# A two-layer kernel whose second input projection takes seven block products instead of eight

## Chip, core and metric

One core of one Trainium2 chip runs one program. The metric is the device time of one launch in microseconds, the median of several runs; less is better. The engines are named as the profile names them: TensorE (PE, its weight loads PEld), VectorE (DVE), ScalarE (ACT), GpSimd (POOL) and SyncE (SP), which here only issues DMAs.

## What is computed

```python
def _attn_ref(x):                        # x: 2 x 3008 x 256
    X = np.fft.fft(x, axis=1)
    X = np.fft.fft(X, axis=2)
    return X.real.astype(np.float32)

def _moe_ref(x, w_in, w_out):            # x: 6016 x 256, w_in: 256 x 2048, w_out: 2048 x 256
    h = x @ w_in
    g = h * (1.0 / (1.0 + np.exp(-h)))
    return (g @ w_out).astype(np.float32)

def _moe2_ref(x, w_in, w_out):           # the same sizes
    h = x @ w_in
    relu6 = np.clip(h + 3.0, 0.0, 6.0)
    g = h * relu6 / 6.0
    return (g @ w_out).astype(np.float32)
```

The reference calls them one after the other: the real part of a two-dimensional Fourier transform, then two layers of two matrix products each. The weights come in as 64-bit floats.

## The kernel before

**Precision.** TensorE multiplies in `float32r`. Each operand is split into a high part (a copy to that type, on ScalarE) and a low part (the operand less the high part, on VectorE or GpSimd), and a product takes three matmuls: high x high, low x high, high x low (`mm3`, lines 243 to 245 in the profile of this kernel). Three such matmuls are called a triple below. All are of 128x128 weights and 502 moving columns (500 in the last chunk).

**Columns and chunks.** The Fourier transform uses the symmetry of a real input: it leaves, for each of 3010 pairs of frequencies, an even and an odd part (`eo`). The pairs are cut into six chunks of 502 (`CHUNKS`); a chunk stands for 2 x 502 tokens.

**Weights.** Each layer has eight pairs `g` of hidden blocks (`whi`, `wlo`: 2 x 512 columns for a pair, 256 of the input projection and 256 of the output projection for each block of 128 hidden units). They are decoded from the bits of the 64-bit floats in a chain of VectorE operations of 1024 columns (`bits_to_float32`). `decoder` and `stage` are generators that hand out one operation after another; `advance` takes from them as many as a credit in ns allows, once per unit, so VectorE's other work stands between them. In layer one `stage` also decodes the first four pairs of layer two, and keeps them in HBM (`w2_d`); the last 14 units of layer one load and split them; the other four are decoded in layer two.

**Layer one.** A unit is one chunk and one hidden block `f`: 96 units, in the order of `segs`, first a few blocks of each chunk (`PARTS`), since the weights are still being decoded, then the rest. `win1` makes the product of the even part into the PSUM tile `ab` (one triple), and VectorE puts `z` aside; `win1_end` adds the odd part's product on top (one triple), and VectorE makes the second half as 2z - ab. `parts` applies SiLU twice for each half on ScalarE, `low` makes the low parts `glo` on GpSimd, and `wout1` makes the output projection into four PSUM accumulators (four triples), three units later (`LAG`). `win1` is called one unit ahead of its `win1_end`. The results stay in SBUF (`y1`).

**Layer two.** A unit is one half of a chunk (502 tokens) and one pair of blocks: 96 units of 24 matmuls. `win2` makes four products (two blocks, two halves of the 256 input rows) into `hp`, of 1004 columns; ScalarE makes relu(h+3), VectorE takes the minimum with 6 and multiplies, ScalarE and VectorE split, and `wout2` follows three units later.

The order on each engine is the order in which this code issues instructions; nothing reorders them. Each engine takes its instructions in order, and one that waits holds up all behind it. All DMAs that matter go through SyncE's one queue.

## Time and profile before

| | |
|---|---|
| median of 3 runs | 996.31 us (993.98 to 997.43) |
| the profiled execution | 994.24 us |
| its span, first to last instruction | 992.5 us |
| mean granted clock of TensorE, of full | 0.993 |
| busy: PE, DVE, ACT, POOL | 975.0, 571.0, 525.1, 255.7 us |
| matmuls | 4416, of them 1152 into `hp` |

The span is one profiled execution; the 1.74 us around it are no part of the trace. The busy time of an engine says how full it is, and not whether anything waits for it; that is seen in the waits and in slices of the span.

### The profile page before, as it was taken

The numbers are of one execution on the slowest core, as the hardware profiler recorded it, in microseconds if no ns is written. First come the engines' busy times: TensorE is split into PE (matmuls) and PEld (weight loads), VectorE is DVE, ScalarE is ACT, GpSimd is POOL, SyncE is SP. The second block draws the span as 40 slices with busy tenths as digits, with TensorE's granted clock in tenths as the row PEclk, the third lists the DMA queues.
The fourth block names the chain that finished last, engine by engine and source line by source line (L and its number), as shares of the span: only waits on it lengthen the run. The fifth ranks groups of instructions, "written<-read, shape, count | busy, mean of one in ns | idle before, by whom it ended". The sixth has DMA issues, their size and how long they took to land.

```text
span 992.5 us, 11053 instructions
## 1 busy us (share of the span) xinstructions
PE 975.0 (98%) x4416; PEld 807.4 (81%) x4416; DVE 571.0 (58%) x630; ACT 525.1 (53%) x751; POOL 255.7 (26%) x197
## 2 busy tenths in 40 slices
PE   9969999999999999999999999999999999999998
PEld 8948778888888888888888888888888888888886
DVE  7787777766767543555976445554444444444433
ACT  3858666676565555665555444344443434444442
POOL 0046665666666666662000000000000000000000
PEclk9979999999999999999999999999999999999999
DMA  9411111001212000021100000000000000000000
GB/s 363 171 53 64 53 44 53 11 0 44 74 64 75 22 32 32 24 104 43 43 1 0 1 22 21 21 21 21 0 22 1 21 1 21 9 12 22 1 21 21
DMA packets 11007, 40.46 MB, mean 41 GB/s; under 512 B 1350, under 2 KB 6348, under 8 KB 8140
## 3 DMA queue, kind: packets, MB, share of 16 engines
q1 hardware_dynamic: 10812, 39.49, 11.0%
q8 instruction: 34, 0.56, 0.2%
q10 hardware_dynamic: 144, 0.27, 0.1%
q14 instruction: 17, 0.14, 0.0%
HBM read 31.48 MB, written 8.27 MB: 40 GB/s over the span
## 4 chain that ended last, share of the span: by engine, by line
PE 92%; DVE 2%; ACT 0%; issue 0%; DVEq 0%
PE y L245 18%; PE y L243 17%; PE y L244 17%; PE hp L245 9%; PE hp L243 9%; PE hp L244 9%; PE ab L245 4%; PE ab L243 4%; PE ab L244 4%; DVE lo L177 0%; DVE hi L175 0%; DVE z L473 0%; DVE h L484 0%; DVE lo L180 0%; DVE wlo L143 0%
## 5 line engine op out<-in xcount | busy, mean ns | idle before, releaser
L560 POOL TENSOR_TENSOR glo<-h,ghi 128x502 fp32r<-128x502 f32 (+1 forms) x192 | 255.3, 1351 | 199.5 <-PE y L244 116.9
L245 PE MATMUL y<-ghi,wlo 128*128 128x502 f32 (+1 forms) x768 | 301.0, 392 | 0.0
L243 PE MATMUL y<-ghi,whi 128*128 128x502 f32 (+1 forms) x768 | 300.9, 392 | 0.0
L244 PE MATMUL y<-glo,whi 128*128 128x502 f32 (+1 forms) x768 | 300.3, 391 | 0.0
L549 DVE SCALAR_TENSOR_TENSOR h<-h,hp 128x1004 f32<-128x1004 f32 (+1 forms) x96 | 115.2, 1200 | 259.3 <-ACT h L548 259.3
L548 ACT ACTIVATE h<-hp,three 128x1004 f32<-128x1004 f32 (+1 forms) x96 | 105.5, 1099 | 160.9 <-PE hp L245 150.2
L244 PEld LDWEIGHTS y<-glo,whi 128*128 128x128 f32 x768 | 145.8, 190 | 31.6
L243 PEld LDWEIGHTS y<-ghi,whi 128*128 128x128 f32 x768 | 145.3, 189 | 31.0
L245 PEld LDWEIGHTS y<-ghi,wlo 128*128 128x128 f32 x768 | 144.9, 189 | 30.6
L496 ACT ACTIVATE ghi<-h 128x1004 fp32r<-128x1004 f32 (+1 forms) x96 | 100.3, 1045 | 125.1 <-DVE h L549 125.1
L245 PE MATMUL hp<-uhi,wlo 128*128 128x502 f32 (+1 forms) x384 | 150.7, 392 | 0.0
L243 PE MATMUL hp<-uhi,whi 128*128 128x502 f32 (+1 forms) x384 | 150.1, 391 | 0.0
L244 PE MATMUL hp<-ulo,whi 128*128 128x502 f32 (+1 forms) x384 | 149.9, 390 | 0.0
L484 DVE SCALAR_TENSOR_TENSOR h<-z,ab 128x502 f32<-128x502 f32 (+1 forms) x96 | 65.0, 677 | 124.9 <-PE ab L245 113.5
L500 ACT ACTIVATE ghi<-ab 128x502 fp32r<-128x502 f32 (+1 forms) x96 | 56.5, 589 | 125.9 <-DVE h L484 125.8
L562 DVE TENSOR_TENSOR glo<-h,ghi 128x1004 fp32r<-128x1004 f32 (+1 forms) x96 | 114.9, 1197 | 0.0
L243 PE MATMUL ab<-xhi,whi 128*128 128x502 f32 (+1 forms) x192 | 76.2, 397 | 10.7 <-DVE z L473 9.9
L244 PEld LDWEIGHTS hp<-ulo,whi 128*128 128x128 f32 x384 | 72.7, 189 | 15.8
L243 PEld LDWEIGHTS hp<-uhi,whi 128*128 128x128 f32 x384 | 72.3, 188 | 15.3
L245 PEld LDWEIGHTS hp<-uhi,wlo 128*128 128x128 f32 x384 | 72.2, 188 | 15.2
L473 DVE SCALAR_TENSOR_TENSOR z<-eb,w_sb,ab 128x502 f32<-128x502 f32 (+1 forms) x96 | 70.8, 738 | 11.8 <-PE ab L245 1.5
L245 PE MATMUL ab<-xhi,wlo 128*128 128x502 f32 (+1 forms) x192 | 75.9, 395 | 0.9 <-DVE wlo L143 0.9
(92 smaller groups left out, 820.9 us busy)
## 6 DMA issues: line engine op xcount, KB each, us to landing
raw<-in_w SPq DMA_DIRECT2D x16, 1024.0 KB, 4.8
x<-in_xh SPq DMA_DIRECT2D x6, 1024.0 KB, 7.1
out<-y SPq DMA_DIRECT2D x20, 251.0 KB, 2.1
eb<-e_d SPq DMA_DIRECT2D x10, 251.0 KB, 3.3
w_d<-ta SPq DMA_DIRECT2D x4, 512.0 KB, 3.0
w<-w_d SPq DMA_DIRECT2D x4, 512.0 KB, 3.8
x<-in_xh SPq DMA_DIRECT2D x3, 512.0 KB
out<-y SPq DMA_DIRECT2D x4, 250.0 KB, 2.0
```

The lines of the kernel that those rows point to most:

```text
L243: T.matmul(o, wh, xhi, start=first, stop=False, **group)
L244: T.matmul(o, wh, xlo, start=False, stop=False, **group)
L245: T.matmul(o, wl, xhi, start=False, stop=last, **group)
L473: V.scalar_tensor_tensor(out=z[:, :n], in0=eb[:, :n], scalar=w128_sb[:, f : f + 1], in1=ab[:, :n], op0=ALU.mult, op1=ALU.add)
L484: V.scalar_tensor_tensor(out=h[:, 0, :n], in0=z[:, :n], scalar=2.0, in1=ab[:, :n], op0=ALU.mult, op1=ALU.subtract)
L496: A.activation(ghi[:, :, :n], h[:, :, :n], AF.Copy)
L500: A.activation(ghi[:, s, :n], src, AF.Silu)
L548: A.activation(h[:, :, :n], hp[:, :, :n], AF.Relu, bias=three)
L549: V.scalar_tensor_tensor(out=h[:, :, :n], in0=h[:, :, :n], scalar=6.0, in1=hp[:, :, :n], op0=ALU.min, op1=ALU.mult)
L560: G.tensor_tensor(out=glo[:, s, :n], in0=h[:, s, :n], in1=ghi[:, s, :n], op=ALU.subtract)
L562: V.tensor_tensor(out=glo[:, :, :n], in0=h[:, :, :n], in1=ghi[:, :, :n], op=ALU.subtract)
```

## The change

**Layer two's input projection.** A unit is now a whole chunk (both halves of 502 tokens) and a pair of blocks: 48 units (`units2`). The 2x2 block product (two hidden blocks by two halves of the input rows, times two halves of the rows by two halves of the tokens) is made from seven products instead of eight, with sums of blocks on both sides. The weight sums (`s1` to `s4`) are made in `block_sums`; those of the moving side (`t1` to `t4`) in `moving`, once per chunk, by VectorE, and split by ScalarE and GpSimd. The products go into four single PSUM tiles, `pa`, `pb`, `pc`, `pd`. `pa` gets three products one after the other, and ScalarE copies it to SBUF after each (`p1`, `u2`, `u3`); `pb` gets two. VectorE adds the pieces together in PSUM. Between the products stand triples of `y` (the output projection of the unit before), handed out by `fill`; a unit has 7 + 8 triples in the order `pa`, `pc`, 2 `y`, `pb`, `pa`, `y`, `pd`, `y`, `pa`, 4 `y`, `pb`. All four low parts of a unit are made on GpSimd.

**Weights.** Six pairs are decoded, summed and split in layer one and wait in HBM in three pieces; the last two are done in units 2 to 8 of layer two.

**Layer one.** `win1` runs two units ahead (`AHEAD`), and `z` has room for four. At the start `wout1` follows two units later instead of three (`CLOSE`). The low part of one half goes to VectorE for odd blocks. The credit per unit is 1500 throughout, instead of 1150 from the fourth on. Partial and full results of a chunk go to HBM and back (`part_d`, `y1_d`).

```diff
+RING = 10
+NEAR = 4
+FIRST = 4
 EARLY = 2
-STAGED = 4
+AHEAD = 2
+CLOSE = 5
+STAGED = 6
...
+    def block_sums(t, x):
+        V.tensor_tensor(out=x[:, 0:128], in0=t[:, 1, 0:128], in1=t[:, 1, 128:256], op=ALU.add)
+        V.tensor_tensor(out=t[:, 1, 0:128], in0=t[:, 0, 0:128], in1=t[:, 1, 0:128], op=ALU.subtract)
+        V.tensor_tensor(out=x[:, 128:256], in0=x[:, 0:128], in1=t[:, 0, 0:128], op=ALU.subtract)
+        V.tensor_tensor(out=x[:, 256:384], in0=t[:, 0, 128:256], in1=x[:, 128:256], op=ALU.subtract)
...
     def add_w2(t, a):
         V.tensor_tensor(out=t, in0=a, in1=t, op=ALU.add)
         yield 1200
+        block_sums(t, a[:, 0])
+        yield 1000
...
+            lows = t.bitcast(F32R), a[:, 0, 0:384].bitcast(F32R)
+            V.tensor_tensor(out=lows[0], in0=t, in1=h, op=ALU.subtract)
+            V.tensor_tensor(out=lows[1], in0=a[:, 0, 0:384], in1=a[:, 1, 0:384], op=ALU.subtract)
+            for dst, src in zip(w2_d[g], (h.bitcast(F32), t, a[:, :, 0:384])):
+                nc.sync.dma_start(dst, src)
...
+            A.activation(h, t, AF.Copy)
+            A.activation(a[:, 1, 0:384].bitcast(F32R), a[:, 0, 0:384], AF.Copy)
...
     def load_w2(g):
-        raws[g] = dp.tile([P, 2, 512], F32, name=f"w2_{g}", tag="raw")
-        nc.sync.dma_start(raws[g], w2_d[g])
-
-    def split_w2(g):
+        if not wx:
+            wx.append(eop.tile([P, NF // 2, 2, 384], F32R, name="wx", tag="eo"))
         weight_tiles(2, g)
-        split(whi[2, g], wlo[2, g], raws.pop(g))
+        for dst, src in zip((whi[2, g], wlo[2, g], wx[0][:, g]), w2_d[g]):
+            nc.sync.dma_start(dst.bitcast(F32), src)
...
+        i = units.index((k, f))
+        if i < 4:
+            if i % 2 == 0:
+                spare[0] = pools[0].tile([P, 2, CHUNK], F32R, name=f"zg{i}", tag="glo").bitcast(F32)
+            return spare[0][:, i % 2]
+        if i == 4:
+            spare[0] = stp.tile([P, 4, CHUNK], F32, name="zs", tag="su", bufs=1)
+        elif i == turn:
+            spare[0] = dp.tile([P, 4, 512], F32, name="zr", tag="raw")
+        return spare[0][:, i % 4]
...
-        z = pools[0].tile([P, CHUNK], F32, name="z", tag="z", bufs=1)
-        product(ab[:, :n], w(1, f, 0), (hi[:, 0, :n], lo[:, 0, :n]), True)
+        z = even_part(k, f)
+        product(ab[:, :n], w(1, f, 0), (hi[:, 0, :n], lo[:, 0, :n]))
...
         glo = pools[0].tile([P, 2, CHUNK], F32R, name="glo", tag="glo")
-        if segs[k][0] == 1:
-            for s in (1, 0):
-                G.tensor_tensor(out=glo[:, s, :n], in0=h[:, s, :n], in1=ghi[:, s, :n], op=ALU.subtract)
-        else:
-            V.tensor_tensor(out=glo[:, :, :n], in0=h[:, :, :n], in1=ghi[:, :, :n], op=ALU.subtract)
+        for s, eng in ((1, G), (0, V if f % 2 else G)):
+            eng.tensor_tensor(out=glo[:, s, :n], in0=h[:, s, :n], in1=ghi[:, s, :n], op=ALU.subtract)
...
                     if fs[0] == 0:
                         A.activation(dst, src, AF.Copy)
                     else:
                         V.tensor_tensor(out=dst, in0=dst, in1=src, op=ALU.add)
...
+                        credit[0] -= 400
+                yield
...
-                pools[1] = tc.alloc_tile_pool(name="psS", bufs=2, space=PSUM, side="right", reuse_waits="tile")
...
+    def moving(k):
...
+        st = stp.tile([P, 2, 2 * CHUNK], F32, name=f"u{k}", tag="su", bufs=1)
+        nc.sync.dma_start(st[:, :, : 2 * n], y1_d[j])
...
+        def rest(name, src):
...
+            G.tensor_tensor(out=lo, in0=src, in1=hi, op=ALU.subtract)
...
+        V.tensor_tensor(out=b12, in0=b22, in1=b12, op=ALU.subtract)
+        high("t1", b11)
+        yield
+        rest("t1", b11)
...
+        V.tensor_tensor(out=b21, in0=b11, in1=b21, op=ALU.subtract)
+        high("t2", b11)
+        yield
...
+
+    def fill(times=1):
+        for _ in range(times):
+            while waiting and next(waiting[0], waiting) is waiting:
+                waiting.pop(0)
...
-        if i >= LAG:
-            k_, f_ = units[i - LAG]
-            (wout1 if segs[k_][0] == 1 else wout2)(k_, f_)
+        lag = LAG - (i < CLOSE)
+        if i >= lag and i != CLOSE:
+            for _ in wout1(*units[i - lag]):
+                pass
+        if EARLY <= i < n1 - AHEAD:
+            win1(*units[i + AHEAD])
...
-        if f == fs[len(fs) // 2 - 1] and k + 1 < len(segs) and k + 1 not in xs:
-            l_, j_, _ = segs[k + 1]
-            xs[k + 1] = split_eo(j_) if l_ == 1 else split_y(j_)
-        if 2 <= i < turn:
-            spare()
...
+        if f == fs[len(fs) // 2] and fs[0]:
+            load_part(k)
+        if k + 1 < len(segs) and k + 1 not in xs and f == fs[1 if k + 2 == len(segs) else len(fs) // 2 - AHEAD]:
+            xs[k + 1] = split_eo(k + 1, segs[k + 1][0])
+        if 2 <= i < turn - AHEAD - 1:
+            advance(steps, 1500)
+        else:
...
+            q, odd = divmod(i - turn, 2)
+            if not odd and 0 <= q < STAGED - 1:
+                load_w2(q)
...
+    def high_part(g, h, i, n):
+        A.activation(g[0][:, i, :n], h[:, i, :n], AF.Copy)
+
+    def low_part(g, h, i, n):
+        G.tensor_tensor(out=g[1][:, i, :n], in0=h[:, i, :n], in1=g[0][:, i, :n], op=ALU.subtract)
...
+    for e, (k, f) in enumerate(units2):
+        j, fs = segs2[k]
+        n = CHUNKS[j][1]
+        u = us[k]
+        while f >= STAGED and len(finished) <= NF + 2 * (f - STAGED):
+            drive(steps2)
+        if e == 0:
+            go(ready, 8)
+        left = len(fs) - 1 - (f - fs[0])
+        more = k + 1 < len(segs2)
+        wh, wl = (t[2, f] for t in (whi, wlo))
+        xl, xh = (wx[0][:, f, i] for i in range(2))
+        a11, a12, s3, a22 = ((wh[:, i, 128 * c : 128 * c + 128], wl[:, i, 128 * c : 128 * c + 128]) for i in range(2) for c in range(2))
+        s1, s2, s4 = ((xh[:, 128 * i : 128 * i + 128], xl[:, 128 * i : 128 * i + 128]) for i in range(3))
+        pa, pc = (pools[1].tile([P, 512], F32, name=f"p{q}", tag=f"p{q}") for q in "ac")
+        product(pa[:, :n], a11, u["b11"])
+        product(pc[:, :n], a12, u["b21"])
+        hy, gy = split_tiles()
+        p1 = snapshot("p1", n)
+        if before:
+            before = (*before, hy, gy)
+            relu(hy, 0, before[3], before[2])
+        fill(2 if e else 4)
+        pb = pools[1].tile([P, 512], F32, name="pb", tag="pb")
+        product(pb[:, :n], s1, u["t1"])
+        V.tensor_tensor(out=pc[:, :n], in0=p1[:, :n], in1=pc[:, :n], op=ALU.add)
+        if before:
+            finish_last(before)
+            before[4][0, 1] = gy, 0
+            waiting.append(wout2(before[0], before[1], before[4]))
+        relu(hy, 1, pc, n)
+        times(hy, 1, pc, n)
+        product(pa[:, :n], s2, u["t2"], False)
+        u2 = snapshot("u2", n)
+        high_part(gy, hy, 1, n)
+        low_part(gy, hy, 1, n)
+        if e > 1:
+            advance(steps2, 1600 if e < FIRST else 2600)
+        if f == fs[0] and e:
+            go(ready, 1)
+        if left == 3 and more:
+            ready = moving(k + 1)
+            next(ready)
+        if more and left < 3:
+            go(ready, (2, 2, 3)[left])
+        fill(1)
+        pd = pools[1].tile([P, 512], F32, name="pd", tag="pd")
+        product(pd[:, :n], a22, u["t4"])
+        fill(1)
+        product(pa[:, :n], s3, u["t3"], False)
+        hx, gx = split_tiles()
+        u3 = snapshot("u3", n)
+        V.tensor_tensor(out=pc[:, :n], in0=u3[:, :n], in1=pb[:, :n], op=ALU.add)
+        V.tensor_tensor(out=pd[:, :n], in0=u3[:, :n], in1=pd[:, :n], op=ALU.subtract)
+        for op in (relu, times):
+            op(hx, 0, pc, n)
+            op(hx, 1, pd, n)
+        for op in (high_part, low_part):
+            op(gx, hx, 0, n)
+            op(gx, hx, 1, n)
+        if more and left == 0:
+            go(ready, 2)
+        fill(4)
+        product(pb[:, :n], s4, u["b22"], False)
+        V.tensor_tensor(out=pd[:, :n], in0=u2[:, :n], in1=pb[:, :n], op=ALU.add)
+        if e == 0:
+            load_w2(STAGED - 1)
+        elif e == 1:
+            begin(2, STAGED)
+        blocks = {(0, 0): (gy, 1), (1, 1): (gx, 0), (1, 0): (gx, 1)}
+        before = (k, f, n, pd, blocks)
```

What moves on the engines is shown at three places. Tile names carry the numbers that the program gives them.

VectorE in an ordinary stretch of layer two, before: `h` is the product with 6.0 taken as minimum, `glo` a low part, `ulo` a low part of a moving operand.

```order
L168 TENSOR_TENSOR ulo5_5146<-y1_619,uhi5_5145 128x1004
L549 SCALAR_TENSOR_TENSOR h_5182<-h_5182,hp_5181 128x1004
L562 TENSOR_TENSOR glo_5198<-h_5149,ghi_5150 128x1004
L549 SCALAR_TENSOR_TENSOR h_5214<-h_5214,hp_5213 128x1004
L562 TENSOR_TENSOR glo_5230<-h_5182,ghi_5183 128x1004
```

And in one unit after:

```order
L863 TENSOR_TENSOR pd_4986<-u2_4972,pb_4959 128x502
L824 TENSOR_TENSOR pc_5034<-p1_5044,pc_5034 128x502
L737 SCALAR_TENSOR_TENSOR h_5041<-h_5041,pd_4986 128x502
L737 SCALAR_TENSOR_TENSOR h_5041<-h_5041,pc_5034 128x502
L851 TENSOR_TENSOR pc_5034<-u3_5089,pb_5053 128x502
L852 TENSOR_TENSOR pd_5076<-u3_5089,pd_5076 128x502
L737 SCALAR_TENSOR_TENSOR h_5086<-h_5086,pc_5034 128x502
L737 SCALAR_TENSOR_TENSOR h_5086<-h_5086,pd_5076 128x502
```

Where a half-unit had two operations of 1004 columns, a unit has eight of 502, four of them sums into the PSUM tiles `pc` and `pd`, and no low parts.

TensorE at the beginning of layer one, before: the end of a unit's products into `ab_629`, then `ab_654`, the first that needs the second weight pair (`whi1_1`, `wlo1_1`), and behind it the first output projection (`y00`; three more triples follow).

```order
L243 MATMUL ab_629<-xhi1_533,whi1_0_499 128x502
L244 MATMUL ab_629<-xlo1_534,whi1_0_499 128x502
L245 MATMUL ab_629<-xhi1_533,wlo1_0_500 128x502
L243 MATMUL ab_654<-xhi1_533,whi1_1_642 128x502
L244 MATMUL ab_654<-xlo1_534,whi1_1_642 128x502
L245 MATMUL ab_654<-xhi1_533,wlo1_1_643 128x502
L243 MATMUL y00_663<-ghi_562,whi1_0_499 128x502
L244 MATMUL y00_663<-glo_620,whi1_0_499 128x502
L245 MATMUL y00_663<-ghi_562,wlo1_0_500 128x502
```

And after, the last two triples of that output projection, the product that needs the second pair (`ab_686`), and the end of the products into `ab_633`:

```order
L293 MATMUL y10_666<-ghi_588,whi1_0_525 128x502
L294 MATMUL y10_666<-glo_652,whi1_0_525 128x502
L295 MATMUL y10_666<-ghi_588,wlo1_0_526 128x502
L293 MATMUL y11_667<-ghi_588,whi1_0_525 128x502
L294 MATMUL y11_667<-glo_652,whi1_0_525 128x502
L295 MATMUL y11_667<-ghi_588,wlo1_0_526 128x502
L293 MATMUL ab_686<-xhi1_559,whi1_1_680 128x502
L294 MATMUL ab_686<-xlo1_560,whi1_1_680 128x502
L295 MATMUL ab_686<-xhi1_559,wlo1_1_681 128x502
L293 MATMUL ab_633<-xhi1_559,whi1_0_525 128x502
L294 MATMUL ab_633<-xlo1_560,whi1_0_525 128x502
L295 MATMUL ab_633<-xhi1_559,wlo1_0_526 128x502
```

The twelve matmuls into `y` stand ahead of the product that needs the new pair, and the triple that stood ahead of it stands behind.

GpSimd's end before: the low parts of the last units of layer one.

```order
L560 TENSOR_TENSOR glo_3811<-h_3763,ghi_3764 128x500 x2
L560 TENSOR_TENSOR glo_3836<-h_3799,ghi_3800 128x500 x2
L560 TENSOR_TENSOR glo_3879<-h_3830,ghi_3831 128x500 x2
L798 UNCONDITIONAL_BRANCH
L798 ISA
```

And after, at a change of chunk in layer two: `glo` is a low part of the hidden values, the others are low parts of the next chunk's moving sums (`t2`, `t4`, `t3`, `b22`).

```order
L745 TENSOR_TENSOR glo_6682<-h_6680,ghi_6681 128x502 x2
L645 TENSOR_TENSOR t2_5_6711<-u5_6453,t2_5_6711 128x502
L745 TENSOR_TENSOR glo_6731<-h_6729,ghi_6730 128x502 x2
L645 TENSOR_TENSOR t4_5_6714<-u5_6453,t4_5_6714 128x502
L645 TENSOR_TENSOR t3_5_6745<-u5_6453,t3_5_6745 128x502
L745 TENSOR_TENSOR glo_6776<-h_6774,ghi_6775 128x502 x2
L645 TENSOR_TENSOR b22_5_6748<-u5_6453,b22_5_6748 128x502
L745 TENSOR_TENSOR glo_6819<-h_6817,ghi_6818 128x502 x2
```

GpSimd works through layer two, and at a change of chunk four more operations stand among its low parts.

## Rows read from the trace of the kernel before

**Rows 1.** The page's first part: busy time, share of the span, instructions.

```profile
PE 975.0 (98%) x4416; PEld 807.4 (81%) x4416; DVE 571.0 (58%) x630; ACT 525.1 (53%) x751; POOL 255.7 (26%) x197
```

**Rows 2.** Windows by stage: stretch, length, busy us (instructions) per engine, granted clock, DMA share, GB/s.

```profile
148.62:463.90 315.28, 314.49 (x1377) 259.35 (x1378) 191.43 (x242) 193.76 (x333) 195.50 (x150) 1.00 0.12 42
...
200.00:300.00 100.00, 100.00 (x439) 82.41 (x438) 67.94 (x86) 62.73 (x109) 64.93 (x50) 1.00 0.13 45
...
464.00:988.50 524.50, 524.50 (x2294) 431.90 (x2292) 266.69 (x242) 234.27 (x234) 0.00 (x0) 1.00 0.04 15
```

**Rows 3.** TensorE's waits: who for whom, us in total, times, longest.

```profile
PE ab L243 <- DVE z L473: 9.9, 5, 3.4
...
PE ab L245 <- DVE wlo L143: 0.9, 1, 0.9
```

**Rows 4.** Timeline of TensorE, 52 to 67 us: start, duration, line, tiles [idle before].

```profile
52.44 0.49 PE L243 MATMUL ab<-xhi,whi 128*128 128x502 f32 x1 [0.80 <-DVE z L473]
...
56.68 0.50 PE L243 MATMUL ab<-xhi,whi 128*128 128x502 f32 x1 [2.60 <-DVE z L473]
...
62.18 0.79 PE L243 MATMUL ab<-xhi,whi 128*128 128x502 f32 x1 [3.38 <-DVE z L473]
...
66.66 0.79 PE L245 MATMUL ab<-xhi,wlo 128*128 128x502 f32 x1 [0.90 <-DVE wlo L143]
```

**Rows 5.** Windows of 5 and 10 us in layer one's beginning.

```profile
60.00:65.00 5.00, 2.08 (x4) 1.29 (x5) 4.86 (x8) 3.15 (x5) 2.56 (x3) 0.50 0.20 51
...
110.00:120.00 10.00, 8.09 (x36) 6.42 (x35) 8.37 (x9) 7.51 (x14) 6.47 (x5) 1.00 0.23 92
...
140.00:150.00 10.00, 8.76 (x39) 6.91 (x38) 8.65 (x9) 6.32 (x11) 7.18 (x6) 1.00 0.31 106
```

**Rows 6.** Groups of instructions by form: shapes, count | busy us, mean ns | idle before.

```profile
L560 POOL TENSOR_TENSOR glo<-h,ghi 128x502 fp32r<-128x502 f32 x160 | 213.8, 1358 | 175.9 <-PE y L244 97.7 <-ACT h L501 78.2
...
L562 DVE TENSOR_TENSOR glo<-h,ghi 128x1004 fp32r<-128x1004 f32 x80 | 95.8, 1198 | 0.0
...
L496 ACT ACTIVATE ghi<-h 128x1004 fp32r<-128x1004 f32 x80 | 83.6, 1045 | 104.9 <-DVE h L549 104.9
...
L484 DVE SCALAR_TENSOR_TENSOR h<-z,ab 128x502 f32<-128x502 f32 x80 | 54.1, 677 | 105.1 <-PE ab L245 94.5 <-issue 6.7 <-POOL glo L560 3.6
...
L501 ACT ACTIVATE h<-ab 128x502 f32<-128x502 f32 x80 | 46.8, 585 | 0.0
...
L117 DVE SCALAR_TENSOR_TENSOR lo<-raw,lo 128x1024 f32<-128x1024 uint32 x10 | 14.4, 1443 | 0.2
...
L586 DVE TENSOR_TENSOR y<-y,y 128x502 f32<-128x502 f32 x20 | 13.0, 675 | 0.0
```

**Rows 7.** Timeline of layer two, 703 to 705 us, three engines.

```profile
703.14 0.40 PE L245 MATMUL hp<-uhi,wlo 128*128 128x502 f32 x1
...
703.62 1.10 ACT L548 ACTIVATE h<-hp,three 128x1004 f32<-128x1004 f32 x1 [2.09 <-PE hp L245]
...
704.76 1.20 DVE L549 SCALAR_TENSOR_TENSOR h<-h,hp 128x1004 f32<-128x1004 f32 x1 [2.07 <-ACT h L548]
```

**Rows 8.** Timelines of VectorE and GpSimd: alone and beside each other.

```profile
56.54 0.68 DVE L175 TENSOR_TENSOR hi<-hi,lo 128x512 f32<-128x512 f32 x1
...
113.73 3.34 POOL L560 TENSOR_TENSOR glo<-h,ghi 128x502 fp32r<-128x502 f32 x2 [0.53 <-ACT h L501]
...
114.18 1.76 DVE L175 TENSOR_TENSOR hi<-hi,lo 128x512 f32<-128x512 f32 x1
...
207.09 2.52 POOL L560 TENSOR_TENSOR glo<-h,ghi 128x502 fp32r<-128x502 f32 x2 [1.61 <-PE y L244]
```

**Rows 9.** The end's timeline, and DMA issues: count, KB each, median us to landing.

```profile
988.84 0.59 ACT L610 ACTIVATE y<-y 128x500 f32<-128x500 f32 x1 [0.78 <-PE y L245]
...
w_d<-ta SPq DMA_DIRECT2D x4, 512.0 KB, 3.0
...
out<-y SPq DMA_DIRECT2D x4, 250.0 KB, 2.0
```

More of the change, by code (lines that the diff above doesn't have):

```diff
@@ new lines, in go @@
+    def go(steps, times):
+        for _ in range(times):
+            next(steps, None)
+    waiting = []
+    def fill(times=1):
+        for _ in range(times):
+            while waiting and next(waiting[0], waiting) is waiting:
+                waiting.pop(0)
+    ready = None
+    for i in range(n1):
+        k, f = units[i]
+        j, fs = segs[k]
+        if i >= EARLY:
+            win1_end(k, f)
+        if i >= 1:
+            low(*units[i - 1])
+        lag = LAG - (i < CLOSE)
[4 more added lines that the diff above has]
+            win1(*units[i + AHEAD])
@@ L669, in body @@
-    for p in (pools[1], psB, pools[0], xsp, eop, yp, dr, dp, wp, per):
+            q, odd = divmod(i - turn, 2)
+            if not odd and 0 <= q < STAGED - 1:
+                load_w2(q)
+        if i == n1 - 1:
+            load_raw(2, w2, STAGED)
+            load_raw(2, w2, STAGED + 1)
+        if i == n1 - 15:
+            ready = moving(0)
+            next(ready)
+        if i >= n1 - 12:
+            next(ready, None)
+    do_later()
+    low(*units[-1])
+    pools[1].release()
+    pools[1] = tc.alloc_tile_pool(name="psS", bufs=1, space=PSUM, side="right", reuse_waits="tile")
@@ new lines, in body, with relu, times @@
+    waiting += [wout1(*units[i]) for i in range(n1 - LAG, n1)]
+    def relu(h, i, c, n):
+        A.activation(h[:, i, :n], c[:, :n], AF.Relu, bias=three)
+    def times(h, i, c, n):
+        V.scalar_tensor_tensor(
+            out=h[:, i, :n], in0=h[:, i, :n], scalar=6.0, in1=c[:, :n], op0=ALU.min, op1=ALU.mult
+        )
+    def high_part(g, h, i, n):
+        A.activation(g[0][:, i, :n], h[:, i, :n], AF.Copy)
+    def low_part(g, h, i, n):
+        G.tensor_tensor(out=g[1][:, i, :n], in0=h[:, i, :n], in1=g[0][:, i, :n], op=ALU.subtract)
@@ L670, in body @@
+    hy, gy = split_tiles()
+    before = (*before, hy, gy)
+    relu(hy, 0, before[3], before[2])
+    finish_last(before)
+    before[4][0, 1] = gy, 0
+    waiting.append(wout2(before[0], before[1], before[4]))
+    while waiting:
+        fill()
+    for p in (pools[1], psB, pools[0], xsp, eop, xq, stp, dr, dp, wp, per):
         p.release()
```

318 lines of the change are left out of this document (172 added, 146 removed).

## The prediction

> **What bounds the kernel now.** I read the page's head first: TensorE is busy 975.0 us, 98% of the span [rows 1]. A busy share alone proves little, so I cut the span into stages [rows 2]: from 200 to 300 us TensorE never pauses and issues 439 matmuls in 100 us, 0.2278 us each; from 464 us to the last matmul at 988.4 it is busy all the time too. So **the price of a matmul here is 0.2278 us, of three that make one product ("a triple") 0.683 us**, and whatever removes matmuls without opening gaps shortens the span by that much each. In those stages VectorE has work for 267 of 524 us, ScalarE for 234 and GpSimd for none: there is room beside TensorE. Then I asked what TensorE waits for at all [rows 3]: 9.9 us in five waits for `z` on VectorE, 0.9 for a weight's low part. The timeline [rows 4] puts 6.8 us of these before 63 us, where the first weights are still being decoded; with TensorE busy for 2.1 of 5 us the granted clock stands there at 0.50 of full, the lower of its two levels, 1.2 GHz. The rest is in the slices 110 to 120 (1.9 us not busy) and 140 to 150 (1.2 us) [rows 5].
>
> **What the change removes.** Of the 4126 rows that TensorE has in the order, 3982 are left: 144 matmuls fewer. That is one product of eight in each of 48 units (8 x 3 x 48 = 1152 matmuls, seven eighths of them left). 144 x 0.2278 = **32.8 us**. Nothing else shrinks; TensorE's operands stay 128x128 weights against 502 columns, so the price per matmul stays.
>
> **What it adds in layer two.** A unit (one pair of hidden blocks, both halves of a chunk) is now 15 triples, 10.25 us, where two units of 5.47 stood. By width and source I price each operation [rows 6]: reading 502 columns from PSUM on ScalarE 0.585 us (the snapshots `p1`, `u2`, `u3` and four `relu`), a copy of 502 out of SBUF at most 0.56 (half of 1.045, and some fixed part), the VectorE products with 6.0 clipped 0.677, GpSimd's low parts 1.28 to 1.36. Per unit: ScalarE 3 x 0.585 + 4 x 0.585 + 4 x 0.56 = 6.3 us; VectorE 4 adds and 4 products = 5.4; GpSimd 4 x 1.3 = 5.2; all below 10.25. The one operation that no row shows is VectorE's add *into* PSUM (`pc`, `pd`). Its nearest row is the add of PSUM and SBUF into SBUF, 0.675 us; I take that, and keep twice it as the other end.
>
> Shares don't settle it, since every engine works in order and the pieces hang on each other. So I walked one unit. An engine starts 0.25 us after a triple's nominal end (the last matmul of `hp` starts at 703.14, ends its 0.228 at 703.37, ScalarE starts at 703.62) and 0.05 after another engine's end [rows 7]. Three chains matter. From the end of the third product into `pa` to the last product into `pb`: 0.25 + 0.585 + 0.675 and two changes of engine, 1.6 us, with four triples of `y` (2.73) to cover it. From the same end to the next unit's product into `pc`: snapshot, add, `relu`, product, 2.9 us, of six triples (4.10). And the longest, once round the unit to the next third product: 0.25, snapshot 0.585, adds 0.675 + 0.675, `relu` 0.585, product 0.677, add 0.675, snapshot 0.585, add 0.675, product 0.677, copy 0.56, `relu` 0.585, snapshot 0.585, with seven changes of engine: **8.1 us, of 14 triples, 9.57**. Each has over a microsecond left: 0 for an ordinary unit. The `y` triples that fill these places belong to the unit before, and their operands are ready about a unit early.
>
> The Trainium skill, Perfetto Trace Analysis (Optimizing Scalar/DVE Operations), gives VectorE a fixed part of some 125 ns on PSUM and 60 on SBUF; by that the add into PSUM would cost at most 0.065 us over its row, an estimate, and the longest chain 8.4 us: the sum would be the same. No run shows it yet.
>
> At a **change of chunk** GpSimd has a queue of its own: after the high parts of the last unit it makes two `glo` halves, `t4`, `t3`, two `glo` halves and `b22` in one row, seven operations. They begin some 3.6 us after the third product (0.25, snapshot, add, `relu`, product, copy and changes of engine) and `b22` is wanted 19 triples and one matmul after it, 13.2 us. Seven at 1.26 (a pair takes 2.52, [rows 8]) end at 12.4, at the mean of 1.358 at 13.1: 0 to little. Six changes: I put 0.5 us for all, up to 5.
>
> **The last two weight pairs** are decoded on VectorE in units 2 to 8: six operations of 1024 columns, at most 1.44 each, the four sums of 128 columns (0.3 each, an estimate: under half of the 0.675 for 502) and two low parts (1.2 and, for 384 columns, 0.5), 11.5 us per pair at most, 3.3 a unit. VectorE is free for about 3.0 us between its second product and the add after `u3`, and the first chain has 1.1 more. On average it fits; where the credit lets one more operation of 1.2 in, 0.4 us is lost, in some three or four units: **+1.5 us** (0 to 8).
>
> **Layer one.** The even parts are begun two units ahead, so VectorE has 6 triples (4.1 us) for `z` instead of 4 (2.7): 1.4 us more. Of the later waits, 1.9 and 1.2 us, 1.4 + 1.2 go: **-2.6** (0 to -3.1). At the start, the first 12 `y` matmuls now stand ahead of the product that waits for a weight's low part until 66.66 us [rows 4], and three matmuls that stood ahead of it now stand behind. TensorE thus does nine matmuls more in time that was idle: 9 x 0.228 = **-2.0** (0 to -3.8 at half the clock). The decoding itself, which ends the wait, is as long as before.
> Against that VectorE gets 48 of GpSimd's 192 low parts (48 x 0.68 = 33 us) and the staging of six pairs instead of four (2 x 8.7, six times 2.9 for sums and low parts, less four splits of 1.2: 29 us). 191.4 of 315.3 us [rows 2] becomes 253, 80%. With 4.1 us of slack for each `z`, and 12 us between a unit's first products and its `y`, I put 0. SyncE's queue carries some 38 MB more (layer one's results through HBM, the pairs in three pieces) at a DMA share that was 0.12 and 0.04, each load issued at least two units ahead of its use: 0.
>
> **The end.** The last copy of 0.59 us stays; the last store is 500 KB in one instead of 250. The nearest rows are 2.0 us for 250 KB and 3.0 for 512 [rows 9]: **+0.9**. The ten triples behind the last unit cover its tail.
>
> **Sum:** -32.8 - 2.0 - 2.6 + 0.5 + 1.5 + 0.9 = -34.5. The profiled execution took 994.24 us (span 992.5 and 1.74 around it): 959.7. The median of the runs, 996.31, lies 2.1 higher; a median of the changed kernel should lie somewhat above its own profile too. I forecast **961 us**.
>
> **Rivals.**
> *Longer links in layer two.* If the add into PSUM costs 1.0 us and each change of engine 0.15, the longest chain grows by 4 x 0.325 + 7 x 0.1 = 2.0 and passes its 9.57 by 0.57: 27 us in 48 units, 988; milder mixes 968 to 988. For it: no row shows the add. Against: every row with PSUM in it lies at 0.58 to 0.74 for 502 columns.
> *VectorE binds layer one.* Alone, the sum of 512 columns takes 0.68 us; beside GpSimd's two low parts it took 1.76 and those 3.34 instead of 2.52 [rows 8]: they exclude each other. The change lets the two halves of a low part start on both engines together, 48 times. At 1.1 us more each, VectorE's 253 us become 305 of 315, and where a unit needs 4.3 us instead of 4.1 for some 70 units, TensorE waits 14 us: 974. Against: GpSimd is busy less, and the credits even it out. The Trainium skill, SBUF — State Buffer (Who interferes with whom), says just that: a VectorE operation with two SBUF inputs and a GpSimd operation that reads SBUF block each other for the whole instruction. The trace agrees, with 1.76 against 0.68 us.
> *Slower than before.* One mechanism: the add into PSUM. Its four places in the longest chain leave 1.4 us; 34.5 us are used up when each unit passes by 0.72 more, at (1.4 + 0.72) / 4 = 0.53 over the row, an add of 1.2 us. At twice the row, 1.35, the chain passes by 1.3: 61 us, 1021.
>
> **Chances.** Forecast (952 to 968) 0.72; longer links 0.10; VectorE in layer one 0.10; slower 0.05; else 0.03. The range, 952 to 976, holds the first, most of the third and a part of the second, 0.8. Within 0.3%, about what a measurement of this kernel can tell from no change, lies almost nothing: faster 0.93, same 0.02, slower 0.05.
>
> **What would show it.** Right: TensorE at 438 or 439 matmuls per 100 us through layer two, about 492 us for its 48 units; no waits for `z` after 100 us; snapshots and products at their rows; the add into PSUM below 0.9 us. Wrong: TensorE waiting in each unit at the product into `pb` or the third into `pa` (longer links), at odd units of layer one for `z` (VectorE), at `b22` on GpSimd at each change of chunk, or VectorE's adds above 1.2 us.

## The result and the profile after

The changed kernel takes **966.14 us** (median of 4 runs, 965.61 to 966.29), the kernel before 996.15 beside it: a ratio of 0.970, interval 0.9682 to 0.9718. The forecast was 961, within 952 to 976. The profiled execution took 966.29 us (span 964.5), 27.95 less than that of before; the sum had 34.5. One of the four executions of the experiment with the even credit alone ran at a granted clock of 0.75 throughout (1151.03 us); its rows are left out, and without it that run's median is 962.79 us instead of 962.88.

The page's first part, of the kernel after (against [rows 1]):

```profile
PE 943.3 (98%) x4272; PEld 779.4 (81%) x4272; DVE 678.8 (70%) x924; ACT 643.3 (67%) x1122; POOL 532.5 (55%) x390
```

TensorE is as full as before, with 144 matmuls fewer; VectorE went from 58% to 70%, GpSimd from 26% to 55%. Windows by stage of the kernel after, as [rows 2] (stretch, length, busy us and instructions of PE, PEld, DVE, ACT, POOL, granted clock, DMA share, GB/s):

```profile
148.62:449.00 300.38, 298.47 (x1305) 245.55 (x1304) 252.37 (x308) 193.87 (x340) 174.11 (x117) 1.00 0.36 132
200.00:300.00 100.00, 99.65 (x436) 81.94 (x435) 93.27 (x109) 66.64 (x114) 58.33 (x38) 1.00 0.39 143
500.00:580.00 80.00, 75.08 (x317) 59.96 (x316) 61.53 (x84) 52.38 (x90) 44.10 (x33) 0.98 0.04 14
...
555.00:560.00 5.00, 2.57 (x9) 1.77 (x8) 4.71 (x8) 1.81 (x3) 1.65 (x2) 0.85 0.00 0
560.00:565.00 5.00, 5.00 (x20) 4.02 (x19) 2.62 (x4) 3.22 (x7) 3.70 (x3) 0.81 0.00 0
...
580.00:959.40 379.40, 379.34 (x1662) 312.77 (x1660) 205.26 (x319) 262.81 (x447) 227.95 (x180) 1.00 0.07 25
```

From 580 us to the last matmul, 379.4 us, TensorE never stops: 0.2283 us a matmul (0.2286 in the last row of [rows 2]). **What is missing stands in the third row**: in 80 us from 500 on it issues 317 matmuls, where 351 go through when nothing waits (first experiment). The waits of TensorE after (who for whom, us in total, times, longest; [rows 3] before):

```profile
PE pb L293 <- DVE pc L851: 4.9, 4, 2.4
PE ab L293 <- DVE zg L525: 2.4, 2, 1.8
PE y L293 <- ACT st L613: 1.8, 2, 1.6
PE y L293 <- ACT eo L401: 1.7, 1, 1.7
PE y L293 <- DVE st L615: 1.7, 2, 1.4
...
PE ab L293 <- DVE zs L525: 0.7, 2, 0.5
```

The waits for `z` (`zg`, `zs`) fell from 9.9 to 3.1 us. Three kinds are new. At the start of layer one `y` waits once for `eo`, for a place in PSUM that ScalarE empties (1.7 us). Later it waits for `st`: the accumulators of the chunk that just ended aren't empty yet (3.5 us). In layer two the second product into `pb` waits for `pc`, VectorE's sum, which reads `pb` first (4.9 us, all between 513 and 572 us).

The sum, stage by stage. The first product of layer two starts at 449.0 instead of 453.1, with 2076 matmuls ahead of it in both traces.

| term | predicted | measured |
|---|---|---|
| 144 matmuls fewer | -32.8 | -32.8 |
| layer one: start -2.0, `z` -2.6, VectorE 0 | -4.6 | -4.1 (453.1 to 449.0) |
| ordinary units | 0 | 0 (after 580 us) |
| changes of chunk | +0.5 | 0 alone (no wait after 580 us) |
| decoding the last two pairs | +1.5 | +7.7 ((351 - 317) x 0.2278) |
| last matmul to the span's end | +0.9 | +1.1 (964.5 - 959.30 against 992.5 - 988.41) |
| sum | -34.5 | -28.1, the profiled executions differ by 27.95 |

The row of layer one is good to about 1 us. Two experiments below (the second and the sixth) leave layer one as the change has it, and from the first product into `ab` to layer two's first product their traces have 403.1 and 403.0 us, the changed kernel's 402.1, that of before 406.4: 3.3 to 4.3 less.

**The operation that no row showed.** One line's operations (ns min/median/max, first and last start), after:

```profile
L851 DVE TENSOR_TENSOR pc<-u,pb x48: 673/685/686, 458.2 to 950.2; 128x502 f32<-128x502 f32 x40, 128x500 f32<-128x500 f32 x8
```

All 48 sums into PSUM take 0.67 to 0.69 us, also the 24 of them during which GpSimd works; the prediction took 0.675 from the nearest row.

**Where layer two loses.** Timelines of three engines in the unit before the longest wait, after (start, duration, engine, line, operation):

```profile
550.21 0.68 DVE L737 SCALAR_TENSOR_TENSOR h<-h,pc 128x502 f32<-128x502 f32 x1 [1.26 <-ACT h L734]
550.81 1.24 DVE L126 SCALAR_TENSOR_TENSOR ta<-raw,ta 128x1024 f32<-128x1024 uint32 x1
552.08 2.18 DVE L209 TENSOR_TENSOR ta<-ta 128x1024 f32<-128x1024 f32 x1
554.30 1.25 DVE L203 TENSOR_TENSOR ta<-ta 128x128 f32<-128x128 f32 x1
555.59 1.21 DVE L204 TENSOR_TENSOR ta<-ta 128x128 f32<-128x128 f32 x1
...
557.24 0.68 DVE L851 TENSOR_TENSOR pc<-u,pb 128x502 f32<-128x502 f32 x1
...
551.63 1.55 POOL L745 TENSOR_TENSOR glo<-h,ghi 128x502 fp32r<-128x502 f32 x1 [0.67 <-ACT ghi L742]
553.15 3.50 POOL L645 TENSOR_TENSOR b<-u,b 128x502 fp32r<-128x502 f32 x2
...
557.98 0.50 PE L293 MATMUL pb<-b,wx 128*128 128x502 f32 x1 [2.43 <-DVE pc L851]
...
559.40 0.62 PE L294 MATMUL pa<-b,whi 128*128 128x502 f32 x1
```

A sum of 128 columns takes 1.25 us beside GpSimd's low parts; two more of its kind in the same unit, left out here, take 0.28 and 0.29. So 3.6 us of work become 6.45, the sum into `pc` comes late, and TensorE stops for 2.43 us. It pays twice: the granted clock, 1.00 until then, is 0.85 and 0.81 in the two windows of 5 us that hold the stop and what follows, a mean of its two levels of 2.4 and 1.2 GHz, and eight matmuls behind the stop stand there with 0.60 to 0.62 us instead of 0.39.

### The profile page after: what moved, and what is told of

The parts are those of the page before. It is cut to its first block, busy times and chain, and to the rows that moved or that the text cites. A ratio compares the mean times of both kernels' runs of the same rounds, so it can differ in the third digit from the quotient of the medians.

```text
span 964.5 us, 11985 instructions
## 1 busy us (share of the span) xinstructions
PE 943.3 (98%) x4272; PEld 779.4 (81%) x4272; DVE 678.8 (70%) x924; ACT 643.3 (67%) x1122; POOL 532.5 (55%) x390
## 4 chain that ended last, share of the span: by engine, by line
PE 77%; DVE 14%; ACT 4%; issue 4%; DMA 1%; DVEq 0%; ACTq 0%
PE y L293 15%; PE y L294 14%; PE y L295 14%; PE pa L293 3%; PE ab L293 3%; PE ab L295 3%; PE ab L294 3%; PE pa L294 3%; PE pa L295 3%; PE pb L293 2%; PE pb L294 2%; PE pb L295 2%; DVE zs L525 1%; DVE h L536 1%; DMA x<-in_xh 1%
## 5 line engine op out<-in xcount | busy, mean ns | idle before, releaser
L745 POOL TENSOR_TENSOR glo<-h,ghi 128x502 fp32r<-128x502 f32 (+1 forms) x192 | 251.1, 1320 | 202.3 <-ACT ghi L742 202.3
L579 POOL TENSOR_TENSOR glo<-h,ghi 128x502 fp32r<-128x502 f32 (+1 forms) x144 | 220.9, 1551 | 215.7 <-ACT h L546 182.4
L742 ACT ACTIVATE ghi<-h 128x502 fp32r<-128x502 f32 (+1 forms) x192 | 118.0, 624 | 51.1 <-DVE h L737 51.1
L737 DVE SCALAR_TENSOR_TENSOR h<-h,pc 128x502 f32<-128x502 f32 (+1 forms) x96 | 65.1, 678 | 71.7 <-ACT h L734 71.7
L851 DVE TENSOR_TENSOR pc<-u,pb 128x502 f32<-128x502 f32 (+1 forms) x48 | 32.8, 684 | 97.1 <-ACT u L788 97.1
L734 ACT ACTIVATE h<-pc,three 128x502 f32<-128x502 f32 (+1 forms) x96 | 64.6, 673 | 49.8 <-DVE pc L851 46.3
L788 ACT ACTIVATE u<-pa 128x502 f32<-128x502 f32 (+1 forms) x96 | 56.6, 590 | 51.0 <-PE pa L295 50.9
L294 PE MATMUL ab<-xlo,whi 128*128 128x502 f32 (+1 forms) x192 | 75.4, 393 | 0.0
L525 DVE SCALAR_TENSOR_TENSOR zs<-eb,w_sb,ab 128x502 f32<-128x502 f32 (+1 forms) x78 | 56.9, 729 | 22.3 <-PE ab L295 22.1
L734 ACT ACTIVATE h<-pd,three 128x502 f32<-128x502 f32 (+1 forms) x96 | 64.7, 674 | 1.6 <-DVE pd L863 1.6
L737 DVE SCALAR_TENSOR_TENSOR h<-h,pd 128x502 f32<-128x502 f32 (+1 forms) x96 | 64.4, 671 | 1.1 <-ACT h L734 1.1
L546 ACT ACTIVATE h<-h 128x502 f32<-128x502 f32 (+1 forms) x96 | 60.0, 625 | 3.0
L545 ACT ACTIVATE ghi<-h 128x502 fp32r<-128x502 f32 (+1 forms) x96 | 60.2, 627 | 0.0
```

The source lines that it names most:

```text
L294: T.matmul(o, wh, xlo, start=False, stop=False, **group)
L525: V.scalar_tensor_tensor(out=z[:, :n], in0=eb[:, :n], scalar=w128_sb[:, f : f + 1], in1=ab[:, :n], op0=ALU.mult, op1=ALU.add)
L545: A.activation(ghi[:, s, :n], src, AF.Silu)
L546: A.activation(h[:, s, :n], src, AF.Silu)
L579: eng.tensor_tensor(out=glo[:, s, :n], in0=h[:, s, :n], in1=ghi[:, s, :n], op=ALU.subtract)
L734: A.activation(h[:, i, :n], c[:, :n], AF.Relu, bias=three)
```

## The experiments

**Theory one:** VectorE's operations that work in SBUF alone are lengthened while GpSimd runs, and that fills the units with decoding in layer two and the chunk ends in layer one. **Theory two:** the credit hands out too much for one unit, whoever runs beside it. For layer one the rival is that VectorE's total of work decides.

**All pairs decoded in layer one.**

```diff
-STAGED = 6
+STAGED = 8
-            advance(steps, 1500)
+            advance(steps, 1650)
-            advance(steps2, 1600 if e < FIRST else 2600)
```

> All eight weight pairs of layer two are decoded in layer one, none in layer two; the credit per unit is 1650 instead of 1500. The changed kernel takes 966.3 us in its profiled run. Both theories of the waits in layer two (VectorE's decoding is lengthened by GpSimd, or it is simply too much for one unit) expect that TensorE's four waits for pc (4.9 us) and the stretch at the lower clock behind them (about 1.9 us) go: layer two 6.8 us shorter, no wait at pb left. They say nothing on layer one, where VectorE gets 17 to 26 us more of work, while it is busy for 132 of 140 us from 160 to 300 and for 109 of 149 after. If there is room, the waits for accumulators grow by 1 to 2 us and the run takes about 961; if VectorE binds layer one, its time goes straight to TensorE and the run takes 970 or more.

975.72 us (0.9798 of before, 0.9779 to 0.9816): the second outcome. Its window and waits, in the views used above:

```profile
500.00:580.00 80.00, 80.00 (x351) 65.94 (x350) 43.65 (x68) 57.13 (x97) 47.92 (x39) 1.00 0.04 14
```

```profile
PE y L293 <- DVE st L615: 7.6, 3, 3.1
PE y L293 <- ACT st L613: 3.8, 2, 2.3
PE ab L293 <- DVE zs L525: 3.5, 6, 0.8
```

Layer two is free of waits, which prices the decoding there at 7.7 us. Layer one loses more than that: from the first `ab` to layer two's first product it takes 421.4 us instead of 402.1, and most of the added waits are at accumulators that VectorE and ScalarE empty late.

**No low parts beside the decoding.**

```diff
     def low_part(g, h, i, n):
+        if quiet[0]:
+            return
...
         def rest(name, src):
+            if k in (1, 2):
+                return
...
+        quiet[0] = e < 10
         hy, gy = split_tiles()
```

> In the first ten units of layer two, and for the moving sums of the second and third segment, GpSimd makes no low parts: the high part stands in for them in the matmuls, so TensorE's work stays the same and this part of the computation is left out. VectorE's decoding of the last two pairs then has no GpSimd beside it. Theory one (VectorE's operations with only SBUF operands are lengthened while GpSimd runs): the two pairs take 8.6 us each instead of 13, no operation of 128 columns above 0.4 us, the waits for pc fall from 4.9 us to at most 1.0, and the run takes about 960. Theory two (the credit hands out too much work in one unit, whoever runs beside it): the waits stay at 3.5 us or more, and the run takes 965 or more.

960.72 us. VectorE's timeline in the same unit, and the window:

```profile
549.01 1.22 DVE L126 SCALAR_TENSOR_TENSOR ta<-raw,ta 128x1024 f32<-128x1024 uint32 x1
550.27 1.23 DVE L209 TENSOR_TENSOR ta<-ta 128x1024 f32<-128x1024 f32 x1
551.53 0.29 DVE L203 TENSOR_TENSOR ta<-ta 128x128 f32<-128x128 f32 x1
```

```profile
500.00:580.00 80.00, 78.56 (x344) 64.53 (x343) 58.16 (x89) 58.31 (x99) 10.62 (x8) 1.00 0.01 1
```

The 24 operations of the two pairs, their rows added up, take 17.6 us instead of 25.8, and the waits for `pc` fall from 4.9 to 1.4 us, in one place. In the window 27 matmuls, 6.2 of the 7.7 us, come back. So without the lengthening most of the waits go, as theory one has it; the 1.4 us, over the expected 1.0, stay with GpSimd's low parts left out. The two theories have no separate shares: spreading the work alone gives back 3.3 us as well (the even credit below), so the waits take both, lengthened operations and many of them in one unit.

**Even parts one unit ahead.**

```diff
-AHEAD = 2
+AHEAD = 1
```

and `win1` called ahead of `wout1`, as before the change.

> Layer one's even parts begin one unit ahead instead of two, at the place where they stood before the change (ahead of the output projection); all else as changed. The prediction priced the second unit at 2.6 us. If that is its worth, the run takes 968.9 us. If VectorE, now busy for 84% of layer one where it was busy for 61% before, needs the longer lead at most units, the waits for z come back more often than before the change: 975 us or more, with most of the time between 75 and 360 us.

979.47 us. Waits of TensorE:

```profile
PE ab L293 <- DVE zs L525: 10.1, 6, 2.3
PE pb L293 <- DVE pc L851: 4.9, 4, 2.4
PE ab L293 <- DVE zg L525: 3.1, 2, 2.5
PE ab L295 <- DVE wlo L152: 2.4, 1, 2.4
```

The lead of a second unit is worth 13.3 us in this kernel, not 2.6: the six waits for `zs` lie between 79 and 348 us, where VectorE has so much more to do than before the change that it comes to `z` late.

**Layer one's low parts on GpSimd alone.**

```diff
-        for s, eng in ((1, G), (0, V if f % 2 else G)):
+        for s, eng in ((1, G), (0, G)):
```

> All low parts of layer one on GpSimd, as before the change; VectorE loses 48 operations that took 40 us. TensorE's new waits in layer one (3.5 us) are for the accumulators, which VectorE or ScalarE empties late at a chunk's end. If VectorE is late because it is too full, its share of them (1.7 us) and the rest of z (0.7) go: 964 us. If GpSimd's operations beside it lengthen it as much as its own low parts did, or if GpSimd (then some 290 of 400 us) is late with the low parts, it is no better: 966 to 970.

962.86 us, 3.3 less than the changed kernel. Of the new waits in layer one only ScalarE's are left:

```profile
PE y L293 <- ACT eo L401: 1.7, 1, 1.7
PE y L293 <- ACT st L613: 1.6, 2, 1.1
```

Those for `zs` (0.7) and for VectorE's `st` (1.7) are gone, and the first product of layer two starts at 445.7. (Who is named in the two waits for VectorE's `st` isn't firm: in the trace of the second experiment, with the same layer one, they are put down to ScalarE's `ghi`. That they go with VectorE's low parts is what this experiment shows.) GpSimd, busy for 107 of 140 us from 160 on, is not late with them. That part of the change cost time.

**No early output projection.**

```diff
-CLOSE = 5
+CLOSE = -1
```

> The output projection follows three units later from the beginning, as before the change; even parts stay two units ahead. The prediction priced the early projection at 2.0 us. In the changed kernel TensorE has issued 24 matmuls more than before between its first ab and 75 us, 5.5 us of its work, and the run with even parts one unit ahead had lost 11 of these, 2.5 us. If the early projection carries the rest, the run takes 969 us (966.1 + 3.0), with a wait for a weight's low part before 70 us as before the change. If its price was right: 968. If the lead of two units carries all of it: 966 to 967.

967.07 us, 0.9 more than the changed kernel. That is no more than traces with one and the same layer one differ by: from the first `ab` to layer two's first product this run takes 403.1 us, where the changed layer one took 402.1, 403.1 and 403.0 in three traces. So the early projection is worth 1 us at most, and perhaps nothing. The windows show a gain that is given back. From 46.5 to 75 us TensorE issues 108 matmuls in the changed kernel, 94 here and 82 before the change; by 100 us it is 208, 204 and 193, since the changed kernel then waits for `z` at 75.28 (0.49) and for `st` at 90.25 (1.58), and this one for neither.

**Three more sums in the chain.**

```diff
+        for _ in range(3):
+            V.tensor_tensor(out=hx[:, 0, :n], in0=u3[:, :n], in1=pb[:, :n], op=ALU.add)
         V.tensor_tensor(out=pc[:, :n], in0=u3[:, :n], in1=pb[:, :n], op=ALU.add)
```

> VectorE does the sum of u3 and pb three times more in each unit of layer two, into a place that is written over, ahead of the sum into pc: the chains through pc get 3 x 0.6 us longer and TensorE's work stays. In the last unit of the changed kernel the sum into pc ends at 950.88 and TensorE's product into pb starts at 952.03: 1.15 us left, as the prediction put it (four triples less 1.6). By that each unit loses 1.8 - 1.15 = 0.65 us at pb, 31 us in all: about 997, as slow as before the change. If the longest chain has less room than the 1.4 us of the prediction, more than that: 1010 and above. If both had more room: below 985.

1039.98 us, 43 more than expected. An ordinary unit, timelines of VectorE and TensorE:

```profile
700.33 2.10 DVE L852 TENSOR_TENSOR h<-u,pb 128x502 f32<-128x502 f32 x3 [2.33 <-ACT u L788]
702.35 0.68 DVE L853 TENSOR_TENSOR pc<-u,pb 128x502 f32<-128x502 f32 x1
...
701.87 0.40 PE L295 MATMUL y<-ghi,wlo 128*128 128x502 f32 x1
703.08 0.50 PE L293 MATMUL pb<-b,wx 128*128 128x502 f32 x1 [0.81 <-DVE pc L853]
703.42 0.39 PE L294 MATMUL pb<-b,wx 128*128 128x502 f32 x1
```

The room in this chain was as predicted: the three sums push 2.02 us, `pb` would have started at 702.10 (701.87 + 0.23) and starts 0.98 later, so 1.04 us were free (1.13 worked out). What the expectation missed is the price: 2.02 instead of 1.8 for three such sums, two matmuls behind each stop, the first into `pb` and the first into `pc`, that take 0.34 and 0.33 us of TensorE's time in place of 0.23, so 11.47 us a unit in place of 10.25 or 58.6 us in 48, and most of the rest in units with decoding or the next chunk's sums in them. The longest chain isn't tested by it, since each stop gives that chain as much room as it takes.

**GpSimd's low parts, with eight or seven pairs in layer one.** The edits of the fourth and the first experiment together; then `STAGED = 7`, credit 1550 in layer one, and 1200 per unit in layer two for the last pair.

> Two edits together: layer one's low parts all on GpSimd (962.9 us by itself) and all eight pairs of layer two decoded in layer one (975.7 by itself, with no wait left in layer two but 16 us of new ones in layer one). Theory: VectorE's fullness decides in layer one. With the low parts gone it has 222 us of 285 from 160 to 445; two more pairs make it 240 to 248, as full as in the changed kernel, whose waits there were 1.7 us. So layer two gains the 6.8 us and layer one loses 1 to 3: 957 to 959. Rival: what costs is VectorE's work beside GpSimd, which is busy for 107 of 140 us there now; then each operation of the two pairs is lengthened and the waits of the first run come back by half: 966 or more.

> Layer one's low parts all on GpSimd, seven pairs decoded in layer one, and the last one in layer two at a credit of 1200 per unit, so one or two operations in a unit. Theory one by its sizes: an operation of 1024 columns is lengthened to at most 2.2 us, two in a unit to 3.4, below the 4.1 us of room: no wait for pc, 6.8 us less in layer two, below 1 us more in layer one: 956 to 958. If even one operation beside GpSimd is too much: above 960.

970.36 us (0.9747, 0.9728 to 0.9767) and 965.11 (0.9695, 0.9677 to 0.9713): both miss the sizes of their theory, and the first comes out as its rival had it. With eight, layer one loses again; its timelines at one of the places:

```profile
366.68 1.78 DVE L124 TENSOR_SCALAR t<-a 128x1024 int32<-128x1024 int32 x1
368.38 0.66 DVE L536 SCALAR_TENSOR_TENSOR h<-zs,ab 128x502 f32<-128x502 f32 x1
...
369.62 2.32 DVE L126 SCALAR_TENSOR_TENSOR t<-raw,t 128x1024 f32<-128x1024 uint32 x1
371.97 2.18 DVE L209 TENSOR_TENSOR t<-a,t 128x1024 f32<-128x1024 f32 x1
...
364.92 10.34 POOL L579 TENSOR_TENSOR glo<-h,ghi 128x502 fp32r<-128x502 f32 x6 [3.32 <-ACT h L546]
```

Both engines are lengthened: 1.78, 2.32 and 2.18 us for what takes 0.69, 1.22 and 1.23 with GpSimd still, and 1.72 us for a low part, 1.26 alone [rows 8]. VectorE is busy for 243.9 us from 160 to 445, as worked out and hardly more than in the changed kernel (240.6), and yet TensorE issues 1202 matmuls there in place of 1238. So VectorE's share of busy time, from which 957 to 959 was worked out, is no measure of its room. The higher credit also acts from the first units on, where VectorE was busy for 79 of 85 us already (363 matmuls from 75 to 160 us in the fourth experiment with 1500, 345 here with 1650); how much of the loss is the credit's and how much the two pairs' isn't told apart. With seven, the credit of 1200 was too small: the last pair wasn't ready, and TensorE waited for its high and its low part:

```profile
567.96 0.79 PE L293 MATMUL pa<-b,whi 128*128 128x502 f32 x1 [2.69 <-ACT whi L170]
570.05 0.79 PE L295 MATMUL pa<-b,wlo 128*128 128x502 f32 x1 [0.89 <-DVE wlo L152]
```

None of the units that hold its operations made `pb` wait, so the miss says nothing against theory one. Layer one was longer too, though: 401.9 us from the first `ab` to layer two's first product, 398.7 in the fourth experiment, where below 1 us was expected.

**The credit spread evenly**, alone, then with GpSimd's low parts, then with the last results stored in 250 KB:

```diff
-            advance(steps2, 1600 if e < FIRST else 2600)
+            advance(steps2, 2250)
...
-        block_sums(t, a[:, 0])
-        yield 1000
+        for _ in block_sums(t, a[:, 0]):
+            yield 250
...
+        if k == len(segs2) - 1:
+            nc.sync.dma_start(out[:, m, c : c + n], st[:, m, s * n : (s + 1) * n])
```

> The same decoding of the last two pairs in the same units of layer two, handed out more evenly: 2250 of credit in every unit instead of 1600 in two and 2600 in five, and the four sums of 128 columns one at a time instead of together. GpSimd's work stays. In the order at most 3.1 us of such operations (by their lengths with no GpSimd beside them) stand in any unit, but for one with 4.3, the two sums of the next chunk among them; before it was 3.6 in one that took 6.45. Theory one (operations are lengthened by up to 1 us for each that GpSimd blocks) with 3 us of room expects one or two short waits, 1 to 1.5 us in all, and no stretch at the lower clock: about 961. Theory two (any amount that fits by its own length costs nothing): below 960.5. If GpSimd lengthens whatever stands there: 965 or more.

> The even credit of the run before, with layer one's low parts all on GpSimd (962.9 us alone). The two act in different stages, so they should add: 962.9 less what the even credit gives by itself, 957 to 958. If they don't add, the place that is left is read from the waits.

> As the run before, and the last results stored in pieces of 250 KB as before the change instead of 500. The prediction priced the larger store at 0.9 us; from TensorE's last matmul to the end of the span it is 4.97 us in the changed kernel and 3.86 in the one before. So 0.9 to 1.1 us less than the run before: 956 to 957.

962.88 us (0.9671, 0.9653 to 0.9688), 960.28 (0.9647, 0.963 to 0.9663) and 959.31 (0.9635, 0.9617 to 0.9654). The even credit gives 3.3 us alone, where 5 were expected, and 2.6 on top of GpSimd's low parts, where 5 to 6 were; from layer two's first product to the end of the span it gives 3.3 there too (515.4 to 512.1). In the second of them two waits for `pc` are left, 1.57 and 1.93 us, where 1 to 1.5 in all were expected. Timelines of VectorE and TensorE at the first:

```profile
495.30 1.41 DVE L114 TENSOR_SCALAR lo<-lo 128x1024 f32<-128x1024 f32 x1
496.75 1.64 DVE L116 TENSOR_SCALAR hi<-lo 128x1024 int32<-128x1024 int32 x1
498.43 1.98 DVE L120 SCALAR_TENSOR_TENSOR hi<-raw,hi 128x1024 int32<-128x1024 int32 x1
...
501.06 0.50 PE L297 MATMUL pb<-b,wx 128*128 128x502 f32 x1 [1.57 <-DVE pc L855]
```

Alone these three take 0.69, 0.69 and 1.22 us: all three were lengthened, 2.6 us of work to 5.0. The split store gave its 1.0 us: from the last matmul's start to the span's end 4.2 instead of 5.2 us. The last of them is the fastest kernel of this study.

**A list of counts in place of the credit**, on top of it:

```diff
-            advance(steps2, 2250)
+            go(steps2, (1, 1, 2, 2, 6, 2, 2, 6, 1, 0)[min(e - 2, 9)])
```

> As the run with the split store (959.3 us), but the decoding of the last two pairs is handed out by a list of counts per unit of layer two instead of by credit: one operation where the next chunk's sums stand too (units 2 and 3), two of 1024 columns elsewhere, nine units in all. The run before still waits 1.57 us in a unit where three operations took 5.0 us beside GpSimd (2.6 alone) and 1.93 us in the one that holds the last five operations and the sums. Theory one: at its lengthened price no unit now holds more than 4.1 us but unit 9 (2.2 + 1.3 + 0.9) and unit 7 (1.9 + 0.6 + 1.3 to 2.0), so at most 0.8 us of waits stay: 956 to 957. If the lengthening isn't what fills the units, the waits move and don't shrink: 959.

961.62 us (0.9648, 0.9621 to 0.9675): no better. Six waits for `pc` of 0.23 to 1.63 us, 4.4 in all. The longest has another cause, ScalarE's timeline in that unit:

```profile
552.36 1.06 ACT L170 ACTIVATE whi<-ta 128x1024 fp32r<-128x1024 f32 x1 [2.13 <-DVE ta L205]
553.33 0.51 ACT L172 ACTIVATE wx<-ta 128x384 fp32r<-128x384 f32 x1
553.74 1.12 ACT L645 ACTIVATE b<-u 128x502 fp32r<-128x502 f32 x2
554.76 0.57 ACT L794 ACTIVATE u<-pa 128x502 f32<-128x502 f32 x1
```

The list lets the copies of the weights be issued in the middle of this unit, and they stand ahead of the snapshot `u` that the sum into `pc` needs. That is the list's own doing; the other five waits, 2.7 us, are in units that hold two to four operations of decoding or of the next chunk's sums, one or two of them lengthened by 0.7 to 1.1 us.

## Why the prediction was right, and where it was off

**Right, with the mechanism:** the price of a matmul where nothing waits, and so the 32.8 us; the sum into PSUM at its nearest row; no loss in an ordinary unit; the room of 1.1 us in the chain to `pb` (1.04 measured); the changes of chunk without decoding; the end (+1.1 for +0.9). The rivals "longer links" and "slower" fall with the 0.685 us.

**Mis-sized: the last two weight pairs.** The step "on average it fits ... +1.5 us (0 to 8)" measured 7.7. It priced the operations of 1024 columns at up to 1.44 us and the small sums at 0.3, 23 us for both pairs, and compared an average of 3.3 us a unit with 4.1 of room. In sum that price was near: 25.8 us measured, 3.7 a unit, still below the room. What failed is the average. Beside GpSimd single operations take up to 2.2 and 1.25 us, and the credit gave one unit six of them, 6.45 us; the prediction had at most one operation of 1.2 too many in a unit. The rows for it stood in the prediction [rows 8], where they were used for layer one only. Without GpSimd's low parts 5.4 us of time come back, shown by the second experiment, and with the same work spread more evenly 3.3, shown by the even credit alone; a part of the price is the lower granted clock behind a stop (0.85 and 0.81 above), which the prediction didn't have.

The Trainium skill, SBUF — State Buffer (Who interferes with whom), also lets VectorE's operations of one SBUF input collide in its two-port modes, and says that one with at most one SBUF input, outside these modes, doesn't contend with GpSimd. The trace agrees: `TENSOR_SCALAR` took 1.42 and 1.64 us beside GpSimd and 0.69 without it, and the sums with one input in PSUM never left 0.67 to 0.69.

**Right in sum, wrong inside: layer one.** -4.6 was predicted and -4.1 measured, but the parts differ, so the agreement is luck. "I put 0" for VectorE's added work was wrong by about 3.3 us: that is what comes back when its 48 low parts go to GpSimd, and it is the rival "VectorE binds layer one" in a milder form, less at `z` than at the accumulators. The early output projection, priced at 2.0, is worth 1 us at most, because its gain is mostly given back by 100 us (26 matmuls ahead of before at 75 us, 14 of them by it; 4 of these are left at 100); and where TensorE waited for a weight's low part, it now waits 1.75 us for a place in PSUM that ScalarE empties (`eo` in the waits above). The lead of two units, priced at 2.6, decides over 13.3, since the stage that it covers became fuller by the same change. What waited before could not show that: a price taken from the old waits is a bound only while the load stays.

**Open:** whether all eight pairs fit in layer one with the credit raised only behind the first units, and whether a better list empties the last 2.7 us in layer two. Neither was tried.

## What to carry to other kernels

Compare work that moves to a busy stage with its room unit by unit, as it will be handed out, and not on average; and price each operation by its longest row beside the engine that will run there. A lead or a buffer that the old profile prices at little may be what carries the added load: take it away in an experiment before calling it cheap. And when work is dealt between two engines that exclude each other, try it whole on the one that isn't waited for.
